# Two attention layers and two SwiGLU layers on one core: Wo's products allowed in the column-tiled form, and TensorE's written-out order changed

## The chip, the cores and the metric

The kernel runs on one core of a Trainium2 chip. The metric is the device time of one execution in microseconds, as a median over runs. A profile is one more execution, with every instruction and DMA packet recorded; matmuls stand under PE, the loads of their stationary operand under PEld.

## The reference, cut to what matters

```
x = x + A(layernorm(x));  x = x + B(layernorm(x))      # twice, same weights both times

A: for each of 64 segments of 32 tokens:               # 2048 tokens, width 576
       h   = concat(mem, segment)                      # 8 memory rows + 32 = 40
       q,k,v = h Wq, h Wk, h Wv                        # 32 heads of 128
       p   = softmax(mask(q k^T / sqrt(128)))          # 40 x 40 for each head
       o   = (p v) Wo                                  # 40 x 576
       mem = o[:8];  out = o[8:]
B: (silu(x w1) * (x w3)) w2                            # 576 -> 4608 -> 576
```

The memory rows make the segments of A a recurrence: a segment's q, k and v need the first eight rows of Wo's result for the segment before. Operands are bf16, sums f32.

## The kernel before

**Steps.** Layer 1's attention runs LAG = 8 segments behind layer 0's, and one step t does segment t of layer 0 and segment t - 8 of layer 1 together (72 steps). Steps 8 to 63 have both layers, so a matmul's moving operand has 2 x 40 = 80 columns; the 8 steps at either end have one, and 40 columns. The FFN (`job`) is done for 128 tokens at a time, four steps' worth, and its pieces are laid between those of attention. In each step the 32 heads go in four groups g of eight.

**The pieces of a group** are nodes that `make_nodes` builds; each has an engine, what it depends on, and the buffers it takes and gives back. TensorE's kinds have a letter each in `KINDS` (line 76): Q and q are the products with Wq and Wk and their tail (576 = 4 x 128 + 64, so the last 64 rows are done apart, as two row tiles side by side); S the scores; T the transposition of the probabilities by TensorE, used in the steps with one layer (with both, a transposing DMA on SP writes PTS from PB); P the product with V (PV); O and o the product with Wo and its tail; X, x, V, v, G, g are those with Wv; F, f, W, w the FFN's; a, b, m, n, p transpositions around the layer norms and the residual. ACT and DVE evict the PSUM banks (`em.qk_ev`, `em.ot_ev` and others), DVE does the softmax with one exponential on ACT, POOL clears PB.

**Wo.** `wo` (line 433) does a group's 8 heads x 4 blocks of 128 of Wo's 576 columns: 32 matmuls that add into the bank y of the step, whose four groups all add into it. `wo_tail` (line 435) does the last 64 columns, the even heads into PSUM partitions 0 to 63 and the odd ones into 64 to 127, two tiles of 64 columns side by side. After the fourth group `y_mem` writes the memory columns of the next step's operand HT, for which the next step's Q and q wait.

**Forms.** Each TensorE node names the forms it allows (`mode`): "full" is the whole 128 x 128 array, "row" two tiles of 64 rows, "col" two tiles of 64 columns, and there are quarter forms for V. Q is "full", q, f and g are "row", S (with two layers) and o are "col"; P, T, F, W, G and the transpositions are "full/col": either. `plan` keeps the forms that all nodes of a run have in common (line 152); when the next node has none of them, the run is closed, all its nodes get the first common form, and a change of form is booked. In "col" `Emitter.mm` (line 623) writes each matmul as a pair: the left 64 columns of the stationary operand at tile position (0, 0), the right 64 at (0, 64), both with the same moving operand. A pair is two matmuls and two weight loads where the full form has one of each.

**The order.** TensorE's order is written out as a string of those letters: `FIRST` (773 nodes, steps 0 to about 15), `FOUR` (208 nodes, four steps and the FFN work that goes with them) repeated 11 times, and `LAST` (664). The letters name kinds; the nodes of a kind are taken in their own order. The other engines' orders follow in `plan`: of what is ready, each takes what can start first, by its table of durations, so they shift when TensorE's order does. The program is fully unrolled.

**The start.** `qk` puts 3 x 4 products of 512 columns with the identity ahead of a step-0 QK whose banks nothing has written yet (u = 0 or 4); each reads one of Wk's four loads. Which of Q and q comes first in the string decides whether the banks are still unwritten.

Of the kernel before, what the change touches and what calls it, by code (L numbers as in the profile page):

```python
# [186 lines left out]
def dve(*ns):  # L187
    return sum(0.065 + n / 960 for n in ns)
# [7 lines left out]
def ew(*ns):  # L196
    return (actc(*ns), dve(*ns))


def ewh(*ns):  # L200
# [2 lines left out]


FIRST = (
    "maqqQqQSqTQQQSqQqqSQTQqSXxVvPPTTOOPoPOooOoQqqqqQQSQVvSqqQQQTQSqqXTSPOPTPOOTooPoxOoQQqqqqQSQvVqSQqQQQSqqTPSTOPoOT"
    "PTOPooOoaQqqQQSQqqVvSqQQQqqqTSQPxTSOPXOToToPPOOooQqqqpQQSVvqqQQnQSFfqqQTQSPfqFSOTFPfWoTOPFTOPoofOoFfqqQQWSFQQqqf"
    "vVqQSTFqfQWQQSqfqFPFTSXfPWTOPOxoTFoPOOffooFVqqvQQWQSQqqfFQqqfFSQTWSPQqfqFQFSTOfPWoTOPFTOPfaOoooFfqqQQvqqSQQWSfVF"
    "qQqQWQTQPqSqTOPbSOxxXTXTPooPOOooQpQQqqqqQSnQSFfqFfQvqVSfFWQqqQfPSFPOOooFfPWOFPofOoFQqqfqQWQSqqqQQQSFSGfgqQQqgfFP"
    "GSWPGfggfFFGOPoOOPWOoooFFffqqQQWSqqQQFvSqfVqQQfFSWqQQqfPPSFFOOPWoOffFPoaoOoWQqqqqQQbSQQQqqSGSgqQQqgPGSOPGggGoPOO"  # L210
    "PooOoQqqqppQQQqvVSSnnQFfqqQQQfqqSFFSPfPwOOWoFPoffFOwPWOooFqqffQQwFWQQqqFSSFffqqQQQQqqwWSSgfGFPGgggGPGOoPOOPWOooo"
    "wFqfqqQQQQSffqqFFSQQwvqVWSFQqqffFQWPwSFffPOPOOowooWFPFOoafQQqqqWSQqqqQQQSwSbQqQgqGSggGPGPOGoPgOPOOooo"
)
FOUR = (
    "QqqqppQvVSQQnnQFqfqFSfqqQQFfqQSWPwPSFffOOowFPWoOPFOooFqfqfQQwQQqqgSWGSFqqfQQQPwQSWFqffqFSGgggGPGPOOwooOPWOooFFqq"
    "ffQQQQSwVvqqfFSQQqqWPFSFfqqfQQwOSWPFFoffPOOWPwOoooFfqqQQqqaSQQqWSQQqqqQQSbwSggGGPGPOggoGPOPOOooo"
)
LAST = (
    "QqqppQQSQqqqvVSQQnqqnQSFPqffQOoSPFOFPwWOFPfooOofQQQqqqfFSwWQQFfqqfFSwWqqQQSGqffgFQFPGgWSwPFggfGOOPoGowPOOooFvfqq"
    "VQQQQSWqqFSFqqffQQQQqqSPwWSFfPOOoWwFffPFPOOooowQWQfqqqFSFfqqQQQWSqqqQQSQbvVVSPwXvxPOPOoOPooOoQQppVqqqQQSqvqnQSnQ"  # L220
    "qffFFQTSqqQTPwFfSPWTOOPFffTFooOPWwOooFffqvVQWFQQqqqQSwSQQfqqFSTFfqqQQWTPwSPFOTOffoPTFoPOOWoowxvXVqqQQFSQqfqqQQSF"
    "QQqqqfQTwPSTSWOPFOffTFPToWoPOwOooFqqfvQQQSQqqfVwWSFFfQqqQTWqSPQQqTOSPbOxooTXPTwPOOooQQpqqqQSqQVvnSqqQQqQSQFfqTFP"
    "STfOPoTOwPTFPOOooofVvqqQQQqqSQQSFfqqFQQSTwqqQTFPffSPOTOwxXooPTFPOOffooFQQqqqqQSQFSfvVqqQQQTqqSQwTPfSOFPFTOwTooPf"
    "POfOooFvVQQqwQqqqSQqqQSQfFTSqQqQfPTSPOOooFTTPPfOOoopwfFFnFwffFFwffFFwwffFfFwFfFwffFfFwFfFwffFFwffFFwffFw"
)
ORDER = FIRST + FOUR * 11 + LAST

# [1 line left out]
class Opt:  # L229

    qk, qkt, sc, tr, pv, wo, wog, vm = 0.0079, -0.0342, 0.0268, 0.1447, 0.0406, 0.2653, 0.0725, 0.1407
# [4 lines left out]
def make_nodes(em, nseg, pools, o=Opt, dma_bw=230e3, load_bw=400e3):  # L236
# [4 lines left out]
    def node(*a, **k):  # L241
        n = Node(*a, **k)
        nodes.append(n)
        return n

    def banks(n=2):
        return [Slot("bank") for _ in range(n)]
# [12 lines left out]
    def load(name, nbytes, prio, fn, deps=()):  # L260
        return node("DMA", nbytes / load_bw, fn, deps=deps, prio=prio, name=name, lat=2.0)
# [7 lines left out]
    ld_o = [load("ldo", kb(1024, 576), g - 6.0, em.load_o(g)) for g in range(NG)]  # L269
# [61 lines left out]
    def paired(t):  # L331

        return role(t) == 1 and both(t) and t + 1 < nst and both(t + 1)
# [12 lines left out]
    def vg_out(t, g, b, deps, row):  # L346

        return [node("AD", (0.56, 0.6), em.v_ev(b[r], row, R64, row, 2 * g + r), deps=deps, prio=t + o.vm + 0.01 * g + (0.05 if row == 0 else 0.0), rel=[b[r]],
                     name="VGe") for r in (0, 1)]
# [12 lines left out]
    def step(t):  # L362
# [6 lines left out]
        mm80 = max(c80 / 2.4 + 2.5, 25.0) / 1000  # L369
# [11 lines left out]
        for g in range(NG):  # L381
            qs, qe = [], []
            for u in (2 * g, 2 * g + 1):
                q = Slot("qkt", users=1)
                b = banks()
                pq = t + o.qk + o.ustep * u
                m_ = node("PE", 32 * mm80, em.qk(t, u, b), deps=hx + hm[:1] + ([ld_h[u // 4]] if t == 0 else []),
                          prio=pq, mode="full", acq=[q] + b, name="QK")
                n = node("PE", 4 * mm80, em.qk_tail(t, u, b), deps=hx + hm + ([ld_h[u // 4]] if t == 0 else []), prio=pq + o.qkt, mode="row",
                         acq=[q] + b, name="QKt")  # L390
                rd += [m_, n]
                me[f"QK{u}"], me[f"QKt{u}"] = m_, n
                for r in (0, 1):
                    qe.append(node("AD", ew(256, 64) if nl == 2 else ew(160), em.qk_ev(t, u, r, q, b[r]), deps=[m_, n], prio=t + o.ustep * u,
                                   rel=[b[r]], name="QKe"))
                qs.append(q)
            s = banks(1)[0]
            sme = Slot("sme")
            pf = t + o.gstep * g
            sc = node("PE", 8 * (0.0312 if nl == 2 else 0.029), em.scores(t, g, qs, s), deps=qe, prio=pf + o.sc, mode="col" if nl == 2 else "full/col", acq=[s, sme], rel=qs, name="SC")  # L400
            a = node("DVE", dve(320), em.sm_add(t, g, s, sme), deps=[sc], prio=pf, rel=[s], name="add")
            m_ = node("DVE", 0.912 if nl == 2 else 0.89, em.sm_max(t, g, sme), deps=[a], prio=pf, name="maxsub")
            c = node("ACT", 0.094 + 320 / 1200, em.sm_exp(t, g, sme), deps=[m_], prio=pf, name="exp")
            pb = Slot(f"pb{g % 2}")
            if g < 2 and t:
                zero = [node("POOL", 0.95, em.pb_zero(pb), deps=zdep[g:g + 1], prio=pf, acq=[pb], name="pbz")]
            else:
                zero = []
            d = node("DVE", 0.623 if nl == 2 else 0.606, em.sm_sum(t, g, sme), deps=[c], prio=pf, name="sum", lat=0.14 if nl == 2 else 0.22)
            w = (1.074 if e else 1.143) if nl == 2 else 0.466  # L410
            pbs = node("DVE", w, em.sm_pb(t, g, sme, pb), deps=[d] + zero, prio=pf, acq=[pb], rel=[sme], name="pb", lat=0.125 if nl == 2 else 0.225)
            pts = Slot("pts")
            if nl == 2 and g < DMA_GROUPS:
                pe_ = [node("DMA", TRD, em.ptd(t, g, pb, pts), deps=[pbs], prio=pf, acq=[pts], rel=[pb], name="TRD", lat=TRL)]
                pts_of[t, g] = pe_[0]
            else:
                bt = banks(nl)
                tr = node("PE", 8 * (0.0258 if nl == 1 else 0.0358), em.ptr(t, g, pb, bt), deps=[pbs], prio=pf + o.tr, mode="full/col", acq=[pts] + bt, rel=[pb], name="TR", lat=0.265)
                pe_ = [node("AD", ew(320), em.pt_ev(t, g, i, b, pts), deps=[tr], prio=pf, rel=[b], name="PTe") for i, b in enumerate(bt)]
                pts_of[t, g] = tr  # L420
            if paired(t):
                hn = [ht_ready[li, s] for s in (t + 1, t + 2) for li in (0, 1) if (li, s) in ht_ready]
                gb, gd = vg_nodes(t, g, hm[:1] + hx + hn, hm[1:])
                vx_ev["VM", t, g] = vg_out(t, g, gb, gd, R64)
            b = banks()
            ot = Slot("ot")
            pv = node("PE", 8 * mm80, em.pv(t, g, pts, b), deps=pe_ + vx_ev["VM", t, g] + vx_ev["VX", t - e, g],
                      prio=pf + o.pv, mode="full/col", acq=b + [ot], rel=[pts], name="PV")
            pvs[t, g] = pv
            if paired(t):  # L430
                vx_ev["VX", t + 1, g] = vg_out(t, g, gb, gd + [pv], 0)
            ote = [node("AD", ew(4 * c80), em.ot_ev(t, g, ab, b[ab], ot), deps=[pv], prio=pf, rel=[b[ab]], name="OTe") for ab in (0, 1)]
            wo = node("PE", 32 * mm80, em.wo(t, g, ot), deps=ote + ([ld_o[g]] if t == 0 else []), prio=t + o.wo + o.wog * g, mode="full",
                      acq=[y] if g == 0 else [], name="WO")
            wot = node("PE", 4 * mm80, em.wo_tail(t, g, ot), deps=[wo], prio=t + o.wo + o.wog * g, mode="col", rel=[ot], name="WOt")
            if g:
                wo.after(wos[0])
            if g:
                wot.after(wots[0])
            wos.append(wo)  # L440
            wots.append(wot)
            me[f"SC{g}"], me[f"PV{g}"], me[f"WO{g}"] = sc, pv, wo
# [950 lines left out]
```

## Time and profile before

| | |
|---|---|
| runs | 2642.74, 2635.89, 2644.21 us; median 2642.74 |
| the profiled execution | 2638.71 us |
| its span, first to last instruction | 2636.9 us |
| mean granted TensorE clock | 0.996 |

The span is what the profile's views divide up. "Busy" of TensorE is the time in which at least one matmul is in flight; each lasts some 200 ns and the next starts long before it ends. In a row of the timeline the first number is the start, the second the time until the last matmul of the row has ended, which overlaps the next row; from the start of one row to the start of the next is the time that the row's work held the engine. A shape such as 128*64 128x80 is rows * columns of the array, then the moving operand.

### The profile page before, as it was taken

The page shows a single profiled execution, that of the slowest core. Times are in us where ns is not written, and L with a number is a line of the kernel's source. Part 1 is how long each engine was busy: PE and PEld are TensorE (multiplying, and loading weights), DVE is VectorE, ACT ScalarE, POOL GpSimd, SP SyncE. Part 2 cuts the span into 40 slices and gives each one's busy share as a digit, 9 for nine tenths or more (in the row PEclk, how much of TensorE's full clock was granted, in tenths as well). Part 3 has the DMA queues.
Part 4 walks back from the last instruction along what each step waited for, and adds up shares of the span by engine and source line. Part 5 has one row for each costly group of instructions (what it writes and reads, how often), then busy time and mean ns, then how long its engine had stood idle before and what let it go on. Part 6 is the DMA issues. An engine that isn't in the chain of part 4 may idle for free.

```text
span 2636.9 us, 134690 instructions
## 1 busy us (share of the span) xinstructions
PE 2574.1 (98%) x60031; PEld 2222.3 (84%) x60031; DVE 2004.5 (76%) x5137; ACT 1264.2 (48%) x3745; POOL 196.7 (7%) x253
## 2 busy tenths in 40 slices
PE   5999999999999999999999999999999999999998
PEld 4788888889888888888888888888888888888886
DVE  4787777887778678777877777787777777777876
ACT  2655553444445454444545444454545445454552
POOL 1100000000000010000001001000100001010000
PEclk9999999999999999999999999999999999999999
DMA  9065755575464656546454654655465464545357
GB/s 324 4 174 135 190 104 147 130 148 139 126 147 115 139 127 155 136 131 151 113 140 116 159 140 128 155 110 139 114 156 143 132 159 94 139 122 146 106 156 247
DMA packets 683207, 371.56 MB, mean 141 GB/s; under 512 B 233753, under 2 KB 672801, under 8 KB 681985
## 3 DMA queue, kind: packets, MB, share of 16 engines
q1 hardware_dynamic: 678944, 355.00, 53.2%
q8 instruction: 469, 7.68, 1.2%
q0 software_dynamic: 3024, 6.93, 0.9%
q10 hardware_dynamic: 656, 1.02, 0.2%
q14 instruction: 114, 0.93, 0.1%
HBM read 306.72 MB, written 2.36 MB: 117 GB/s over the span
## 4 chain that ended last, share of the span: by engine, by line
PE 91%; DVE 4%; DMA 3%; issue 1%; ACT 1%; ACTq 0%; DVEq 0%; SPq 0%
PE bank L627 91%; DMA PTS<-PB 2%; DVE HTT L633 1%; DVE PB L633 1%; DVE STAT L633 1%; DMA WV<-in_A_Wv_dram 0%; DVE SME L633 0%; DMA W<-in_A_Wk_dram 0%; DVE V L633 0%; DVE QKT L633 0%; DMA W2C<-in_B_w_dram 0%; DVE XR L633 0%; ACT HTT L630 0%; ACT HT L630 0%; DVE LNS L633 0%
## 5 line engine op out<-in xcount | busy, mean ns | idle before, releaser
L627 PEld LDWEIGHTS <-W 128*128 128x128 bf16 (+2 forms) x32920 | 1261.8, 101 | 119.8 <-issue 67.8
L627 PE MATMUL bank<-HT,W 128*128 128x80 bf16 (+3 forms) x23040 | 795.2, 197 | 21.3 <-ACT HT L630 8.2
L627 PE MATMUL bank<-XTB,W 128*64 128x256 bf16 (+5 forms) x9880 | 658.4, 264 | 2.1 <-issue 1.3
L630 ACT ACTIVATE QKT<-bank 128x256 bf16<-128x256 f32 (+4 forms) x1676 | 385.1, 309 | 302.9 <-PE bank L627 296.5
L627 PE MATMUL bank<-OT,WO 128*128 128x80 bf16 (+3 forms) x11520 | 411.6, 198 | 2.5 <-issue 1.9
L627 PEld LDWEIGHTS <-WO 128*128 128x128 bf16 (+1 forms) x11520 | 383.2, 102 | 29.9 <-issue 16.3
L630 ACT ACTIVATE V<-bank 64x512 bf16<-64x512 f32 (+1 forms) x603 | 338.0, 584 | 137.4 <-PE bank L627 131.4
L627 PE MATMUL bank<-WV,HT 128*32 128x512 bf16 (+4 forms) x3576 | 363.5, 384 | 0.3 <-issue 0.2
L627 PE MATMUL bank<-W2C,HTT 128*64 128x288 bf16 (+1 forms) x3440 | 323.8, 287 | 0.5 <-DMA W2C<-in_B_w_dram 0.5
L630 ACT ACTIVATE HTT<-bank 128x512 bf16<-128x512 f32 (+1 forms) x322 | 172.6, 551 | 300.1 <-PE bank L627 299.1
L633 DVE TENSOR_REDUCE STAT<-SME 104x8 f32<-104x320 f32 (+1 forms) x576 | 274.9, 477 | 28.2 <-ACT SME L630 21.2
L633 DVE TENSOR_TENSOR PB<-SME,STAT 40x128 bf16<-40x128 f32 (+4 forms) x912 | 274.8, 335 | 9.3 <-DMA PTS<-PB 0.5
L627 PEld LDWEIGHTS <-HT 128*32 128x32 bf16 (+4 forms) x3576 | 149.2, 99 | 147.7 <-issue 37.8
L633 DVE SCALAR_TENSOR_TENSOR HTT<-HTT,bank 128x512 bf16<-128x512 bf16 (+1 forms) x322 | 201.0, 624 | 94.4 <-ACT HTT L630 91.6
L627 PEld LDWEIGHTS <-HTT 128*64 128x64 bf16 (+1 forms) x3512 | 233.1, 106 | 31.2 <-DVE HTT L633 4.1
L1047 POOL MEMSET PB<- 128x1024 bf16 x142 | 135.0, 952 | 1657.0 <-DMA PTS<-PB 1114.3
L633 DVE SCALAR_TENSOR_TENSOR XR<-bank,XR 128x288 f32<-128x288 f32 x574 | 240.0, 447 | 20.3 <-PE bank L627 17.2
L630 ACT ACTIVATE OT<-bank 128x320 bf16<-128x320 f32 (+1 forms) x383 | 144.4, 404 | 214.5 <-PE bank L627 185.3
L630 ACT ACTIVATE SME<-SME 104x320 f32<-104x320 f32 (+1 forms) x288 | 135.5, 470 | 194.3 <-DVE SME L633 192.4
L633 DVE TENSOR_TENSOR HTT<-HTT,bank 128x512 bf16<-128x512 bf16 (+1 forms) x322 | 203.3, 631 | 28.5 <-PE bank L627 1.4
L633 DVE CAST V<-bank 64x512 bf16<-64x512 f32 (+1 forms) x261 | 178.9, 686 | 40.1 <-PE bank L627 34.9
L633 DVE TENSOR_TENSOR SME<-bank,maskb 104x320 f32<-104x320 f32 (+1 forms) x288 | 138.5, 482 | 53.8 <-PE bank L627 50.1
(59 smaller groups left out, 1383.5 us busy)
## 6 DMA issues: line engine op xcount, KB each, us to landing
W<-in_B_w_dram SPq DMA_DIRECT2D x608, 256.0 KB, 3.6
W2C<-in_B_w_dram SPq DMA_DIRECT2D x304, 288.0 KB, 3.4
W<-in_B_w_dram SPq DMA_DIRECT2D x608, 32.0 KB, 3.4
W<-in_B_w_dram SPq DMA_DIRECT2D x8, 1024.0 KB, 12.6
W<-in_A_Wq_dram SPq DMA_DIRECT2D x9, 512.0 KB, 9.9
WO<-in_A_Wo_dram SPq DMA_DIRECT2D x4, 1152.0 KB, 19.1
XR<-in_A_x_dram POOLq DMA_DIRECT2D x16, 288.0 KB, 3.1
WV<-in_B_w_dram SPq DMA_DIRECT2D x4, 1152.0 KB, 7.5
```

The source lines that it names most:

```text
L627: self.ch("PE", self.nc.tensor.matmul(out, lhsT=lhsT, rhs=rhs, start=start, stop=stop, skip_group_check=True, **k))
L630: self.ch("ACT", self.nc.scalar.activation(*a, **k))
L633: self.ch("DVE", getattr(self.nc.vector, fn_)(*a, **k))
L1047: return lambda n: self.ch("POOL", self.nc.gpsimd.memset(self.pbt(pb), 0.0))
```

## The change

One node's list of forms, and the three strings of TensorE's order.

```
-            wo = node("PE", 32 * mm80, em.wo(t, g, ot), deps=ote + ([ld_o[g]] if t == 0 else []), prio=t + o.wo + o.wog * g, mode="full",
+            wo = node("PE", 32 * mm80, em.wo(t, g, ot), deps=ote + ([ld_o[g]] if t == 0 else []), prio=t + o.wo + o.wog * g, mode="full/col",
...
 FOUR = (
-    "QqqqppQvVSQQnnQFqfqFSfqqQQFfqQSWPwPSFffOOowFPWoOPFOooFqfqfQQwQQqqgSWGSFqqfQQQPwQSWFqffqFSGgggGPGPOOwooOPWOooFFqq"
-    "ffQQQQSwVvqqfFSQQqqWPFSFfqqfQQwOSWPFFoffPOOWPwOoooFfqqQQqqaSQQqWSQQqqqQQSbwSggGGPGPOggoGPOPOOooo"
+    "QqqqppQvVSQQnnQFfqqFSqfqQQFfqQSWPwPSFffOoOwoPFWOoPFOoFqqffQQwQQqqgSWGSFfqqQQQPwQSWFqffqFSGgggGPGOPOWoOPFoOwooFfq"
+    "qfQQQQSWVvfqqFSQQqqwPFSFqqffQQOSWwPFFPffOOooWPwOooFfqqQQqqaSQQqqWSQQqqQQSbwSggGGPGPOoggGPOoPOOoo"
...
 FIRST = (
-    "maqqQqQSqTQQQSqQqqSQTQqSXxVvPPTTOOPoPOooOoQqqqqQQSQVvSqqQQQTQSqqXTSPOPTPOOTooPoxOoQQqqqqQSQvVqSQqQQQSqqTPSTOPoOT"
+    "maQqqqQqSQQQTqqSQqSqTQQSvVXxPPTTOoPOoOPoOoQqqvqqQQSQVqqSQQQSqQTqPSTXPTOOPoTOPxooOoQQqqqqQSQVvSqqQQqQSqQTPSTOPoTO"
```

`FIRST` and `LAST` change throughout in the same way. The counts of each kind stay: the same nodes in another order. With the new list, a run of neighbours that holds O and also S or o is no longer closed at O: the whole run, and with it P, F, W, G and T where they stand in it, can take the column form. `wo` itself is not edited; in the column form `Emitter.mm` writes its 32 matmuls as 32 pairs.

More of the change, by code (lines that the diff above doesn't have):

```diff
@@ L205 @@
 FIRST = (
-    "maqqQqQSqTQQQSqQqqSQTQqSXxVvPPTTOOPoPOooOoQqqqqQQSQVvSqqQQQTQSqqXTSPOPTPOOTooPoxOoQQqqqqQSQvVqSQqQQQSqqTPSTOPoOT"
[L207 to L210, printed above, removed]
@@ L211 @@
-    "PooOoQqqqppQQQqvVSSnnQFfqqQQQfqqSFFSPfPwOOWoFPoffFOwPWOooFqqffQQwFWQQqqFSSFffqqQQQQqqwWSSgfGFPGgggGPGOoPOOPWOooo"
-    "wFqfqqQQQQSffqqFFSQQwvqVWSFQqqffFQWPwSFffPOPOOowooWFPFOoafQQqqqWSQqqqQQQSwSbQqQgqGSggGPGPOGoPgOPOOooo"
+    "maQqqqQqSQQQTqqSQqSqTQQSvVXxPPTTOoPOoOPoOoQqqvqqQQSQVqqSQQQSqQTqPSTXPTOOPoTOPxooOoQQqqqqQSQVvSqqQQqQSqQTPSTOPoTO"
+    "PoTOPoaOoQQqqqqQSQVvqqSQQqTQSQqxPTSOPXOToToPPOoOoQqqqpQQSVvqqqQQnSQFfqQTSQPFfqOSTFfPWTOPFooTOPoffOoFQWqqqQQSQqqf"
+    "vVQTFSFQqfqQQSqWPFSXffFTTxWPOTPOoFoPOOooFffvVqqqQQWQSFqqffQFSQWQQqfqqQSTFTfPFSOPWoTOPaFTOPfooOoFfqqQQqqvSQQWSVFf"
@@ L213 @@
+    "QqQqTWqqQQPSTOPboSOxXTXTPxoPOoOoQpQqqqqQQSnQSFfqFfvqQVSFfqQWqQfPSFPFOofOPoWOFfPoOoFQqfqqQQSQQQqqqWSGSFfgqqQQFfgP"
+    "GSWPGFffggFGOoPOWPoOoOoFFqqffQQWqqSQQvFSqfVQQqWSFfqqQQfPPSFOOoFoPWOfFPfoaOoWQqqqqQQbSQQQqqSGSgqQQqgPGSOPGggoGPOO"
+    "PooOoQQppQqqqqQVSSnqvnQFqfqQQQSFqffPFOSWwPoFFffPOoOwPWOooFqqfqQQwQQqWSSffqQFFQQQqqqwSWFgffGSFPGgggGPGOoPOPOFWwoo"
+    "OoFqffqQQQQSwFqfqqQQWqvVSSFqffFQQqwPWSFFffPOOWooPwOPFOoofaQQqqWSqqqQQQQSqwSbQQqqgGSggGPGPOgGoPOPOOooo"
 )
 FOUR = (
-    "QqqqppQvVSQQnnQFqfqFSfqqQQFfqQSWPwPSFffOOowFPWoOPFOooFqfqfQQwQQqqgSWGSFqqfQQQPwQSWFqffqFSGgggGPGPOOwooOPWOooFFqq"
@@ L216 @@
-    "ffQQQQSwVvqqfFSQQqqWPFSFfqqfQQwOSWPFFoffPOOWPwOoooFfqqQQqqaSQQqWSQQqqqQQSbwSggGGPGPOggoGPOPOOooo"
+    "QqqqppQvVSQQnnQFfqqFSqfqQQFfqQSWPwPSFffOoOwoPFWOoPFOoFqqffQQwQQqqgSWGSFfqqQQQPwQSWFqffqFSGgggGPGOPOWoOPFoOwooFfq"
+    "qfQQQQSWVvfqqFSQQqqwPFSFqqffQQOSWwPFFPffOOooWPwOooFfqqQQqqaSQQqqWSQQqqQQSbwSggGGPGPOoggGPOoPOOoo"
 )
 LAST = (
-    "QqqppQQSQqqqvVSQQnqqnQSFPqffQOoSPFOFPwWOFPfooOofQQQqqqfFSwWQQFfqqfFSwWqqQQSGqffgFQFPGgWSwPFggfGOOPoGowPOOooFvfqq"
-    "VQQQQSWqqFSFqqffQQQQqqSPwWSFfPOOoWwFffPFPOOooowQWQfqqqFSFfqqQQQWSqqqQQSQbvVVSPwXvxPOPOoOPooOoQQppVqqqQQSqvqnQSnQ"
@@ L221 @@
[L221 to L224, printed above, removed]
+    "QqqppQQSQqqqvVSQQqqnnQSFfqfPQOSoPFOFPWwOFPofoOofQQQqqfFSwQWQqfqqFSFqqfqQQQWwSSFgfgfGFPGWwOPFgfgGGoPOwPOOoooWVvfq"
@@ new lines @@
+    "qFQQQSQQqfqqFSFqqfqQQQSPwWSfFPFOOWwoPffFPoOOoowWFqfqQQQSFfqqqQQSWqqQQqSQVvVPSbwXvxPOPoOOPooOoQQppVqqqQQSqqvnQSnQ"
+    "qffFFTqQSQPWFTqfwPTOSOFPffFOoooTWPwOoFqqfvVQQWSFQfqqqQwQSFqfqfFQQTSTQWqwPSFOPoTFPTOoPOOooffxXVvqWQQqqqQSQwQSQqqF"
+    "qqffFQSTQWwSTPFTOffPFoPwTOWPoOoOoFvqqfQQQSQfqqVwWSFFfQQqqTWTSqqQPQOoPSbOXToxPTwPOoOoQqqqpQQSQvqVSQnqqQQTfSFQqqFP"
+    "STfPOToOowPTFPOoOofVvqqQQQQSqqQSFqqfqQQFSTwPQffqTOSPFTOXxooPTwPOFOoofFQqqfqQQSQqfVvSFTQQqqQSPqqQwSTFPfFTOOofPwTO"
+    "PooOoFfvVqfQQqwSQqQqqqQSFQQTQqSqSTPPOFfOToTPPOOooopfwfFFnFwffFFwffFFwwfFffFwFffFwFfFwffFFwffFfFwFfFwffFw"
```

## Prediction

> **What bounds the kernel now.** I read the page's engine row first, then the chain that ended last, then TensorE's waits, then its timeline.
>
> ```profile
> PE 2574.1 (98%) x60031; PEld 2222.3 (84%) x60031; DVE 2004.5 (76%) x5137; ACT 1264.2 (48%) x3745; POOL 196.7 (7%) x253
> ...
> q8 instruction: 469, 7.68, 1.2%
> ...
> PE 91%; DVE 4%; DMA 3%; issue 1%; ACT 1%; ACTq 0%; DVEq 0%; SPq 0%
> ```
> ```profile
> PE bank L627 <- issue: 9.2, 15, 1.6
> PE bank L627 <- ACT HT L630: 8.2, 20, 1.9
> PE bank L627 <- DMA W<-in_A_Wk_dram: 6.4, 4, 3.2
> PE bank L627 <- DMA PTS<-PB: 5.0, 11, 1.4
> ```
> ```profile
> 0.00:236.00 236.00, 197.83 (x5760) 164.60 (x5761) 164.60 (x444) 112.92 (x318) 24.20 (x39) 0.96 0.51 163
> 236.00:2365.00 2129.00, 2117.20 (x47778) 1839.63 (x47775) 1634.43 (x4178) 1026.29 (x3083) 156.38 (x195) 1.00 0.56 136
> 2365.00:2636.90 271.90, 259.09 (x6507) 218.11 (x6502) 205.46 (x517) 125.04 (x346) 16.16 (x19) 0.99 0.54 161
> ```
>
> TensorE is busy 98% of the span and holds 91% of the chain. The three stages of the windows view (first number: length; second: PE busy and count) are the steps with one layer at the start, the steps with both, and one layer again: PE idles 38, 12 and 13 us. So what the change does to the length of TensorE's stream, it does to the time, nearly one for one. The row of queue q8 is TensorE's own code: 7.68 MB in 469 packets is 16,384 bytes each, and 469 x 256 = 120,064, against 2 x 60,031 = 120,062 matmuls and weight loads. One packet therefore brings 256 instructions of 64 bytes: a **block** of 128 matmuls with their weight loads. I need this below.
>
> **What the change does to TensorE's order.** I counted both orders by the rule in `plan` (a run of neighbours takes a form that all allow). Before, all 288 WO groups are full. After, 263 are column-tiled: 210 of 80 columns (210 x 32 = 6720 products become pairs) and 53 of 40 columns (1696 pairs). The neighbours they join turn with them: 26 more PV and 13 more TR groups at 40 columns, and at 80 or more columns 121 PV, nearly all VG, and most FF and W2. Changes of form fall from 1269 to 1085. TensorE's matmuls rise from 60,031 to 71,176, so its blocks from 469 to 556. DVE and ACT get the same work, a few evictions of it exchanged between them. SP and POOL issue the same DMAs; on SP 292 places of 985 differ, such as a load of XN that now stands elsewhere among the FFN weights. TensorE's waits on DMAs behind the start are the 5.0 us for PTS in the row above, and I put this reordering at nothing, between losing the 5.0 and doubling it.
>
> **Term 1: changes of form.**
>
> ```profile
> 1164.20 1.91 PE L627 MATMUL bank<-XTB,W 128*64 128x256 bf16 x32
> 1165.95 0.45 PE L627 MATMUL bank<-PTS,V 128*64 128x80 bf16 x16
> 1166.23 1.15 PE L627 MATMUL bank<-W2C,HTT 128*64 128x288 bf16 x16
> 1167.22 1.56 PE L627 MATMUL bank<-OT,WO 128*64 128x80 bf16 x40
> 1168.61 0.45 PE L627 MATMUL bank<-PTS,V 128*128 128x80 bf16 x8
> 1168.90 1.91 PE L627 MATMUL bank<-XTB,W 128*128 128x256 bf16 x16
> 1170.65 1.72 PE L627 MATMUL bank<-OT,WO 128*128 128x80 bf16 x48
> 1172.20 1.92 PE L627 MATMUL bank<-XTB,W 128*64 128x256 bf16 x32
> 1174.05 0.32 PE L627 MATMUL bank<-HT,W 64*128 64x80 bf16 x8
> 1174.20 0.38 PE L627 MATMUL bank<-XTB,W 64*128 64x256 bf16 x4
> 1174.42 0.31 PE L627 MATMUL bank<-HT,W 64*128 64x80 bf16 x8
> 1174.56 0.38 PE L627 MATMUL bank<-XTB,W 64*128 64x256 bf16 x4
> 1174.87 2.47 PE L627 MATMUL bank<-HT,W 128*128 128x80 bf16 x64
> 1177.18 1.15 PE L627 MATMUL bank<-W2C,HTT 128*128 128x288 bf16 x8
> ```
>
> Matmuls overlap, so I measure from one row's start to the next row's, never by the busy time. FF in columns, followed by its own form: 1165.95 - 1164.20 = 1.75; followed by row tiles: 1174.05 - 1172.20 = 1.85. FFt without a change behind it 0.22, with one 0.31. A change costs 0.09 to 0.10; I take 0.095. 184 fewer: **-17.5 us**. The first pairs after a change are slower too: WO's 48 rows, 32 full and 16 in 8 pairs, take 1.55 = 32 x 0.036 + 0.095 + 8 x 0.035 + 0.02, and 64 full ones after a change 2.31 instead of 2.30. 45 fewer entries into columns at 0.02 and 135 fewer into full at 0.01: **-2.2 us**.
>
> **Term 2: a pair against a full product.** At 80 columns PV takes 0.28 for 8 pairs (35 ns) and 0.29 for 8 full (36 ns); FF 1.75 in both forms. So 6720 WO pairs cost nothing more, as long as a run goes on like its first 8 pairs. At 40 columns it differs:
>
> ```profile
> 2525.51 0.35 PE L627 MATMUL bank<-ident,PB 104*128 104x40 bf16 x8
> 2525.71 1.05 PE L627 MATMUL bank<-XTB,W 128*128 128x128 bf16 x16
> ...
> 2527.74 0.96 PE L627 MATMUL bank<-OT,WO 128*128 128x40 bf16 x32
> 2528.54 0.35 PE L627 MATMUL bank<-ident,PB 104*128 104x40 bf16 x8
> ...
> 2532.79 0.43 PE L627 MATMUL bank<-OT,WO 128*64 128x40 bf16 x16
> 2533.07 0.41 PE L627 MATMUL bank<-PTS,V 128*64 128x40 bf16 x16
> 2533.32 0.41 PE L627 MATMUL bank<-ident,PB 104*64 104x40 bf16 x16
> 2533.57 1.06 PE L627 MATMUL bank<-XTB,W 128*64 128x128 bf16 x32
> ```
>
> Full: 0.80 / 32 = 25 ns, and 0.20 for 8. Column pairs: 0.25 / 8 = 31 ns. 1696 x 6 ns = 10.2, and 39 groups of PV and TR x 0.05 = 2.0: **+12.2 us**. Terms 1 and 2 together: -17.5 - 2.2 + 12.2 = **-7.5 us**.
>
> At the start the first QK now opens its banks itself, and so brings 12 more warm-up products:
>
> ```profile
> 32.47 2.89 PE L627 MATMUL bank<-W,ident 128*128 128x512 bf16 x12
> ```
>
> They cost 0 to 2.9 us; I take 0, because they stand where TensorE waits 6.4 us for Wk (row above), each behind one of its four loads.
>
> **Term 3: the supply of instructions.** This one decides. In the last stage the timeline shows waits that no semaphore explains:
>
> ```profile
> 2538.00 0.27 PE L627 MATMUL bank<-OT,WO 128*64 128x40 bf16 x6 [0.82 <-issue]
> 2538.12 1.06 PE L627 MATMUL bank<-XTB,W 128*64 128x128 bf16 x32
> 2539.11 2.20 PE L627 MATMUL bank<-HT,W 128*128 128x40 bf16 x90
> 2541.75 1.15 PE L627 MATMUL bank<-HT,W 64*128 64x40 bf16 x38 [0.44 <-issue]
> ```
>
> Between the two waits stand 6 + 32 + 90 = 128 matmuls, exactly one block. TensorE had run out of code, got a block at 2538.00, and although it idled again at the end it had the next one only at 2541.75: a starved block costs **3.75 us**. A block of full products of 80 columns lasts 128 x 0.036 = 4.6 us, and the middle stage's mean block 2129 / (47778 / 128) = 5.7 us, so the supply is just covered there. A block of column pairs of 80 columns does the same work in 64 pairs = **2.3 us**: 1.4 us short. The changed order has runs such as POoPOOoo, 124 pairs of 80 columns in a row (two blocks), in each of 11 repeats; before, the longest such run is 24 pairs.
>
> I laid both orders out at the rows' prices (0.095 a change, 36 and 31 ns a pair) and cut them into blocks. Taking each block by itself, 33 blocks of before fall short of 3.75 us, by 12.3 us together; if two neighbours may share, by 5.2. The trace has 9.2 (the row "issue"), in between. After: 158 blocks, by 128 us alone and 84 shared (38 in the first stage with its 31 ns pairs, 26 in the 11 repeats, 20 in the last). Added: 128 - 9.2 = 118 at most, 84 - 9.2 = 74 at least by this count; placed as before's 9.2 lies, 99. I take 87, nearer the shared end, since most short blocks of the repeats have a long neighbour to share with. While TensorE starves, the other engines catch up, so waits of the other two kinds go: 8.2 + 5.0 = **-13**. Sum: -7.5 + 87 - 13 = **+66 us**.
>
> [...]
>
> [...]
>
> The profiled execution took 2638.71 us (span 2636.9 and 1.8 around it); the median of the runs is 2642.74, between 2635.89 and 2644.21, so the base may be off by 4. 2638.7 + 66 = **2705 us**.
>
> **Rivals.**
> - *Changes of form alone.* The supply keeps up after all: -7.5, **2631 us**, the side of faster. For it: in 2129 us of the middle stage PE idles 12 us, and 3.75 was measured while data DMAs ran; against it: the waits 128 matmuls apart. It decides where a starved block takes 2.6 us or less: the shared count is then about 5 us and the single one 17, which the saved changes pay. Chance 0.10; half of it beyond 0.3% (7.9 us), which is about what a measurement of this kernel can tell from no change. [...]
> - *Slow pairs.* A long run is held by its weight loads, two of 31 ns one after the other, 62 ns a pair: 6720 x 26 ns = +175 on top of -7.5, **2806 us**. Against it: 35 ns in 8 pairs. It loses from 37 ns a pair on. Chance 0.03.
> - *Half covered.* Deeper buffering in the repeats, the added wait is 0 to 15 us: within 8 us of before, **2639 us**. Chance 0.03. It needs the 26 us of the repeats gone and most of the 40-column waits with them; but if eight neighbours shared, the count is still 24 against 1.2, so +15 and 2654, which I count to the forecast's low end.
> - *Forecast*, supply-bound in short blocks: chance 0.84, between 2654 and, with all 118 us and no wait saved, 2749; with blocks at 4.2 us more.
>
> **Numbers.** Faster by over 0.3%: 0.05 (half of the first rival). Within: 0.05 + 0.03 = 0.08. Slower: 0.84 + 0.03 = 0.87. The range, 2652 to 2760, leaves out the first rival, the slow pairs, and the ends of the forecast.
>
> **What would show it.** Right: the row "issue" among TensorE's waits grows from 9.2 to 70 us or more, the waits lie 128 matmuls apart, behind runs of WO in 128*64 form; PE's share falls below 97%; packets of q8 near 556; the timeline still has 35 to 36 ns a pair inside WO at 80 columns and 31 at 40. Wrong: "issue" stays near 9 and the span drops by 7 to 8 (the first rival), or WO's pairs run at 40 ns or more with no gaps (slow pairs). The size fails if blocks starve at other than 3.75 us in the middle stage, where data DMAs are as busy as anywhere (0.56).

## The result, and the profile after

The changed kernel takes 2739.46 us (median, 2735.73 to 2744.64) against 2641.94 us for the kernel before (2635.89 to 2644.21): a ratio of 1.0374, with a 95% interval from 1.0349 to 1.0399, or 97.5 us more. The forecast was 2705, its range 2652 to 2760. The profiled execution took 2735.73 us with a span of 2733.9, 97.0 us over the span of before.

From the page of after, the engine row, the row of q8 and the chain, each to be held against its row of before:

```profile
PE 2609.5 (95%) x71173; PEld 2275.5 (83%) x71176; DVE 2007.0 (73%) x5137; ACT 1268.2 (46%) x3745; POOL 196.7 (7%) x253
...
q8 instruction: 556, 9.11, 1.4%
...
PE 91%; issue 3%; DMA 3%; DVE 2%; ACT 1%; SPq 0%; ACTq 0%; DVEq 0%
```

TensorE was idle for 2636.9 - 2574.1 = 62.8 us before and is for 2733.9 - 2609.5 = 124.4 us after: 61.6 of the 97 us are idle time of the engine that sets the end. The other engines have the same work in more time. TensorE's waits in after say what it waits for (in total, times, longest):

```profile
PE bank L627 <- issue: 71.1, 86, 2.8
...
PE bank L627 <- DMA W<-in_A_Wk_dram: 6.6, 2, 4.3
PE bank L627 <- ACT HT L630: 6.4, 20, 0.3
...
PE bank L627 <- DMA PTS<-PB: 2.9, 6, 1.1
```

"Issue", the wait that no semaphore explains, went from 9.2 us in 15 waits to 71.1 us in 86 (+61.9), as much as the added idle time. HT and PTS fell by 3.9 us together. The groups by their shapes show whose waits these are (the last column is idle time ahead of the group, and its releaser). Wo's products of 80 columns before:

```profile
L627 PE MATMUL bank<-OT,WO 128*128 128x80 bf16 x7168 | 285.2, 202 | 0.2
```

Wo's column pairs after, with the pairs of its tail:

```profile
L627 PE MATMUL bank<-OT,WO 128*64 128x80 bf16 x15232 | 319.3, 202 | 24.9 <-issue 21.1 <-DVE V L633 2.2
L627 PE MATMUL bank<-OT,WO 128*64 128x40 bf16 x3904 | 85.9, 194 | 23.4 <-issue 23.3
```

44 of the 71 us stand ahead of Wo's column pairs themselves. How far apart the waits lie is seen in the timeline of after, in one of the repeats:

```profile
438.92 1.05 PE L627 MATMUL bank<-OT,WO 128*64 128x80 bf16 x47 [0.43 <-issue]
439.77 1.18 PE L627 MATMUL bank<-W2C,HTT 128*64 128x288 bf16 x16
440.75 0.48 PE L627 MATMUL bank<-PTS,V 128*64 128x80 bf16 x16
441.03 1.18 PE L627 MATMUL bank<-W2C,HTT 128*64 128x288 bf16 x16
442.01 0.77 PE L627 MATMUL bank<-OT,WO 128*64 128x80 bf16 x33
443.21 1.05 PE L627 MATMUL bank<-OT,WO 128*64 128x80 bf16 x47 [0.42 <-issue]
```

47 + 16 + 16 + 16 + 33 = 128 matmuls between two waits: one block, and 4.29 us. The same in the first stage, where the pairs have 40 columns:

```profile
191.74 1.29 PE L627 MATMUL bank<-OT,WO 128*64 128x40 bf16 x70 [0.80 <-issue]
192.87 1.06 PE L627 MATMUL bank<-XTB,W 128*64 128x128 bf16 x32
193.77 0.28 PE L627 MATMUL bank<-OT,WO 128*64 128x40 bf16 x8
193.89 0.41 PE L627 MATMUL bank<-PTS,V 128*64 128x40 bf16 x16
194.14 0.19 PE L627 MATMUL bank<-OT,WO 128*64 128x40 bf16 x2
197.11 2.65 PE L627 MATMUL bank<-OT,WO 128*64 128x40 bf16 x128 [2.78 <-issue]
200.84 0.56 PE L627 MATMUL bank<-OT,WO 128*64 128x40 bf16 x14 [1.08 <-issue]
```

Blocks of 5.37 and 3.73 us. In all, the trace has 27 places where two waits of the row "issue" stand 128 matmuls apart; they last from 3.45 us, 4.3 in the median, and 95% of them up to 5.3. With the waits that are too short for that row there are 37 such places, 4.0 us in the median. Most other distances between such waits are multiples of 128, or one or two matmuls short of one: TensorE's queue also holds some 110 semaphore instructions, which would account for that.

The three stages of after, by windows (length; PE busy and count; the other engines; granted clock, DMA share, GB/s):

```profile
0.00:236.00 236.00, 192.50 (x6105) 159.91 (x6108) 143.81 (x387) 98.44 (x271) 21.70 (x36) 0.89 0.47 153
236.00:2365.00 2129.00, 2078.59 (x55637) 1828.15 (x55636) 1603.66 (x4100) 1010.99 (x3026) 152.04 (x189) 1.00 0.56 133
2365.00:2733.90 368.90, 338.45 (x9445) 287.39 (x9439) 259.49 (x651) 158.72 (x450) 22.94 (x28) 0.97 0.50 144
```

The stretches are those of before, so their ends cut the work elsewhere. Two things are to be seen: in the middle stretch TensorE idles 50 us instead of 12, and in the outer ones the granted clock fell, from 0.96 to 0.89 and from 0.99 to 0.97. The prediction had not foreseen the second.

To share out the 97 us I took, over the whole trace, the time from each matmul's start to the next one's and set it against what is usual for that form at full clock. What exceeds it by over 0.3 us is a wait; the rest belongs to a change of form, to half clock, or to the products themselves. In us:

| | before | after | difference |
|---|---|---|---|
| waits of TensorE | 84.6 | 173.0 | +88.4 |
| lost to half clock, waits apart | 2.6 | 10.9 | +8.3 |
| changes of form, beyond the usual distance | 109.6 | 87.8 | -21.8 |
| the products themselves | 2425.7 | 2448.2 | +22.5 |
| ahead of the first matmul | 10.7 | 10.1 | -0.6 |

The waits are larger here than in the row "issue" because that row starts to count where the last matmul has ended, about 0.2 us after the next could have started. Which of the first two rows a wait at half clock is put under is a matter of counting: a second count, with the mean distance of each form as the usual one, gives +80 and +16 for them and -22 and +24 for the next two. The first two rows are surer as a sum than each by itself.

### The profile page after: what moved, and what is told of

It is laid out like the page before. It is cut to its first block, busy times and chain, and to the rows that moved or that the text cites. A ratio compares the mean times of both kernels' runs of the same rounds, so it can differ in the third digit from the quotient of the medians.

```text
span 2733.9 us, 156952 instructions
## 1 busy us (share of the span) xinstructions
PE 2609.5 (95%) x71173; PEld 2275.5 (83%) x71176; DVE 2007.0 (73%) x5137; ACT 1268.2 (46%) x3745; POOL 196.7 (7%) x253
## 4 chain that ended last, share of the span: by engine, by line
PE 91%; issue 3%; DMA 3%; DVE 2%; ACT 1%; SPq 0%; ACTq 0%; DVEq 0%
PE bank L627 91%; DMA PTS<-PB 1%; DMA W<-in_B_w_dram 1%; DMA W<-in_A_Wk_dram 1%; DVE HTT L633 1%; DVE V L633 0%; DVE PB L633 0%; DVE STAT L633 0%; DMA XN<-in_A_x_dram 0%; DVE SME L633 0%; DMA W2C<-in_B_w_dram 0%; DVE QKT L633 0%; ACT HT L630 0%; ACT HTT L630 0%; DVE OT L633 0%
## 5 line engine op out<-in xcount | busy, mean ns | idle before, releaser
L627 PE MATMUL bank<-XTB,W 128*64 128x256 bf16 (+5 forms) x10232 | 667.3, 265 | 9.0 <-issue 6.3
L630 ACT ACTIVATE QKT<-bank 128x192 bf16<-128x192 f32 (+4 forms) x1678 | 383.4, 310 | 280.8 <-PE bank L627 276.5
L627 PE MATMUL bank<-OT,WO 128*64 128x80 bf16 (+2 forms) x19936 | 434.2, 200 | 48.3 <-issue 44.4
L627 PEld LDWEIGHTS <-WO 128*64 128x64 bf16 (+1 forms) x19936 | 409.1, 114 | 68.0 <-issue 63.0
L627 PE MATMUL bank<-WV,HT 128*64 128x512 bf16 (+3 forms) x4070 | 365.5, 387 | 1.2 <-issue 1.2
L627 PEld LDWEIGHTS <-HT 128*64 128x64 bf16 (+3 forms) x4072 | 156.6, 102 | 149.3 <-issue 45.8
L627 PEld LDWEIGHTS <-HTT 128*64 128x64 bf16 (+1 forms) x4096 | 246.8, 109 | 28.4 <-issue 5.0
```

The lines of the kernel that those rows point to most:

```text
L627: self.ch("PE", self.nc.tensor.matmul(out, lhsT=lhsT, rhs=rhs, start=start, stop=stop, skip_group_check=True, **k))
L630: self.ch("ACT", self.nc.scalar.activation(*a, **k))
```

## The experiments

**Theory:** TensorE runs out of instructions wherever a block of 128 matmuls has less array time than the supply of a block takes; the column form hurts because it makes two instructions of one. **Rivals:** the new order is to blame; or the column form is slow in itself.

**The form alone.** The kernel before, with the order that it had, and one word changed:

```
-            wo = node("PE", 32 * mm80, em.wo(t, g, ot), deps=ote + ([ld_o[g]] if t == 0 else []), prio=t + o.wo + o.wog * g, mode="full",
+            wo = node("PE", 32 * mm80, em.wo(t, g, ot), deps=ote + ([ld_o[g]] if t == 0 else []), prio=t + o.wo + o.wog * g, mode="full/col",
```

> The order of before, with Wo allowed the column form (the one line of the diff outside the order): 247 of 288 WO products go in columns, 70,160 matmuls in 548 blocks of 128, 1092 changes of form. Supply theory: the count of short blocks at 3.75 us is 130 us alone and 82 shared (after 128 and 84), so as slow as after: about 2730 us (2715 to 2745), TensorE's wait 'issue' 60 to 80 us. Rival, the new order is to blame: the form alone only saves changes, 2631 to 2645 us, 'issue' near 9 us. Rival, slow column pairs: near 2730 too, but without gaps, 'issue' near 9 and more than 36 ns a pair in the timeline.

2746.75 us (2735.24 to 2749.05), ratio 1.0387, interval 1.0363 to 1.0410: as slow as after (2 us above the expected range). TensorE's first wait in it:

```profile
PE bank L627 <- issue: 75.5, 100, 2.4
```

The loss needs no new order. By the shares of the table above: waits +94, half clock +5, changes -19, products +17.

**The order alone.** After, with that word changed back.

> The order of after, with Wo held to full products: 60,355 matmuls in 471.5 blocks, 1417 changes of form instead of 1269. Supply theory: the changes cost 148 x 0.095 = 14 us, pairs of PV and TR fall back to full, the short blocks amount to 10.3 us alone and 3.7 shared (before 12.3 and 5.2): 2650 to 2660 us, 'issue' 5 to 12 us. Rival, the new order is to blame: 2690 us or more.

2663.31 us (2662.10 to 2667.18), ratio 1.0082, interval 1.0067 to 1.0097: 21 us over before and 3 above the expected range. By the shares, waits +0.5 and changes +15 (148 more), products +6, half clock +2.5; "issue" is 7.7 us. An order made for the column form is worth little without it, but it isn't what costs 97 us.

**Half the pairs' instructions.** After, in which a pair of Wo's issues its left half alone (the first product of a step excepted), so that half of Wo's result is left out:

```
+                    first = g == 0 and hl == 0 and db == 0
+                    if n.mode == "col" and not first:
+                        self.mm(yT[0:R64, db, :], self.T.WO[:, self.head(g, hl), db * P:db * P + R64], OT[:, hl, :], False, False,
+                                tile_position=(0, 0))
+                        continue
...
```

> After, with the right 64 columns of Wo's column products left out (all but the first of a step), so that each pair is one instruction pair fewer: the same order, the same changes of form, and the same time in the array if the two columns of a pair run side by side, but 62,700 matmuls in 490 blocks instead of 71,152 in 556. This leaves out half of the Wo products. Supply theory: the short blocks fall to 14.5 us alone and 7.1 shared, 'issue' to 8 to 18 us, and the time to 2631 to 2655 us. Rival, the column form itself is slow (weight loads, or the way its products stand): the time stays at 2700 us or more with few instructions too. Rival, a column costs by itself and not by the pair: the 263 products would run in half their time and the time would fall by over 100 us below before.

2641.80 us (2638.98 to 2647.15), ratio 0.9998, interval 0.9988 to 1.0007. The profile of this kernel, its waits and its two groups of Wo's columns:

```profile
PE bank L627 <- issue: 8.2, 10, 2.9
```
```profile
L627 PE MATMUL bank<-OT,WO 128*64 128x80 bf16 x8554 | 311.8, 202 | 1.5 <-issue 0.9 <-ACT OT L630 0.3
L627 PE MATMUL bank<-OT,WO 128*64 128x40 bf16 x2215 | 79.3, 191 | 1.2 <-issue 1.0
```

This speaks against both rivals. Order, forms and changes of form are those of after; the groups are still in flight for 311.8 us with 8554 matmuls instead of 319.3 with 15,232, so one column takes the time of a pair, and the column form is not slow in itself. The number of instructions fell, with it the work of the right 64 columns, and "issue" went from 71.1 to 8.2 us and the time down by 98 us.

**The supply by itself.** All of the computation is left out. Stages of 16 blocks of one product each (the calls are set several to a line here); a pair has `tile_position=(0, 0)` and `(0, 64)`. This kernel and the two others of products alone were run once each.

```
    stage(80, False, 16); stage(80, True, 16); stage(128, True, 16)     # columns, in pairs, blocks
    stage(40, False, 16); stage(40, True, 16); stage(512, False, 1)
    traffic(18); stage(80, True, 16); stage(512, False, 1)
    traffic(18); stage(80, False, 16)
```

> All of the computation is left out; TensorE runs stages of 16 blocks of 128 matmuls each on data that lies there, with nothing that waits for another engine: full products of 80 columns, column pairs of 80, column pairs of 128, full of 40, column pairs of 40, and then, with 18 loads of FFN weights running, column pairs of 80 and full of 80. Supply theory: a block of column pairs of 80 takes 3.4 to 3.8 us instead of the 2.3 us of its array time, with a gap at each block's end and 35 ns a pair inside; the pairs of 40 the same 3.4 to 3.8 us instead of 2.0; full products of 80 take 4.6 us without gaps and pairs of 128 3.6 us with almost none; full ones of 40 3.3 to 3.8. With loads running the pairs take 3.8 to 4.5 us a block. Rival, slow column pairs: the pairs of 80 are slow evenly, over 40 ns each, without gaps. Rival, the supply keeps up: 2.3 us a block. The granted clock: if starvation brings half speed, the stages of pairs have a lower clock than those of full products; otherwise both have 1.00 after the start.

The timeline of that kernel, from its full products of 80 columns into the pairs, and later full products of 40 columns and the pairs under the loads:

```profile
17.21 79.86 PE L627 MATMUL bank<-WO,W 128*128 128x80 bf16 x2271 [17.21 <-DMA WO<-in_A_Wo_dram]
97.91 2.48 PE L627 MATMUL bank<-WO,W 128*64 128x80 bf16 x128 [0.84 <-issue]
101.91 2.48 PE L627 MATMUL bank<-WO,W 128*64 128x80 bf16 x128 [1.52 <-issue]
105.36 2.48 PE L627 MATMUL bank<-WO,W 128*64 128x80 bf16 x128 [0.97 <-issue]
...
149.01 68.01 PE L627 MATMUL bank<-WO,W 128*64 128x80 bf16 x2432 [1.52 <-issue]
217.38 6.82 PE L627 MATMUL bank<-WO,W 128*128 128x40 bf16 x256 [0.36 <-issue]
224.56 6.82 PE L627 MATMUL bank<-WO,W 128*128 128x40 bf16 x256 [0.36 <-issue]
...
361.26 2.48 PE L627 MATMUL bank<-WO,W 128*64 128x80 bf16 x128 [2.09 <-issue]
...
426.57 28.57 PE L627 MATMUL bank<-WO,W 128*64 128x80 bf16 x163 [1.53 <-issue]
```

Full products of 80 columns run without a wait (under the loads with a single one, of 0.23 us). The pairs wait at every 128th matmul: 14 blocks in 149.01 - 97.91 = 51.1 us, 3.65 us a block, of which the pairs themselves take 2.3. With the loads, 14 blocks take 426.57 - 361.26 = 65.3 us, 4.66 a block (some of it half clock, below), more than the 4.5 expected at most. Pairs of 128 columns (in the row from 149.01) have next to no waits, as expected. Full products of 40 columns, 3.3 us a block in the array, wait too: 12 blocks take 261.36 - 217.38 = 44.0 us, 3.67 a block. So it is a block's array time that counts, and not the column form.

The trace also has the time of each packet of q8, and these show where the 3.65 us go. There is one packet for each block (114 for 14,596 matmuls), and no two are under way at once. In the 14 blocks of pairs from 97.91 on, the packet of the next block starts 1.0 to 1.6 us after the first matmul of the running one (1.1 in the median), takes 0.9 to 1.4 us (1.0), and the next block's first matmul comes 1.3 to 1.5 us after the packet's end (1.4). With the loads only the first of the three parts grows in the median, to 2.1 us. So a block's supply is one fetch at a time, 1.1 + 1.0 + 1.4 = 3.5 us by the medians from one block's first matmul to the next one's, and while a block runs only the packet of the next one comes; bandwidth is not what is short (DMA share 0.02 in the quiet stage, in the windows below).

**Only the two-layer steps.** After, with Wo free in the steps of 80 columns alone: `mode="full/col" if nl == 2 else "full"`.

> After, with Wo held to full products in the steps of one layer (40 columns) and free in those of two (80 columns): 210 WO products in columns, 68,987 matmuls, 1157 changes of form. The short blocks at 3.75 us: 42 us shared, 82 alone. Supply theory: 26 of the 42 lie in the repeats, whose added time stays at about 28 us as in after, and the first and last stage give back most of what they lost, in waits (first stage 38 to 13 us shared, last 20 to 4) and in granted clock (0.994 or more instead of 0.986): 2665 to 2690 us, 'issue' 35 to 55 us. Rival, the 80-column runs do no harm and all is due to the 40-column form: 2630 to 2645 us. Rival, what costs is the new order in the first and last stage: 2720 us or more.

2697.22 us (2688.15 to 2704.48), ratio 1.0213, interval 1.0187 to 1.0238: 55 us of the 97 stay, above the expected range by 7. By the shares, waits +53, half clock +4, products +10, changes -13. "Issue" is 47.2 us in 76 waits. So the steps of both kinds pay: more than half of the loss comes from pairs of 80 columns, and the granted clock of the first stage is back at 0.97.

**Few pairs, chosen.** The order of before, with Wo allowed the column form in the two-layer steps; the forms are chosen for the whole order at once, each instruction more at a price:

```
+            more = EXTRA.get(n.name, 5) if m == "col" and "full" in n.forms else 0
+            row[m] = best[src[m]] + (0.11 if src[m] != m else 0.0) + lam * more
...
+    reform(order, 0.005, 0.002)
```

> The order of before. Each of TensorE's products that can take both forms has its form chosen for the whole order at once, with 0.11 us for a change and 5 ns (first and last stage) or 2 ns (repeats) for each instruction pair more; WO may go in columns in the steps of two layers. 49 of 288 WO products do, 61,106 matmuls in 477 blocks, 1227 changes of form instead of 1269. Supply theory: changes -4 us, pairs at 40 columns that turn full -2, short blocks 4.6 us shared and 19 alone (before 5.2 and 12.3), so 2630 to 2645 us, the same or up to 8 us faster. Rival, any WO in columns costs about as after's do (97 us for 263): 49 would add 18 us.

2642.51 us (2634.20 to 2649.77), ratio 0.9998, interval 0.9986 to 1.0010, "issue" 7.6 us. 49 groups of Wo in columns, chosen so, do no harm (the rival had 18 us more), and the 4 us of changes don't show. No version here beats the kernel before.

**What a neighbour lends.** Only products again, pairs (64 are 128 matmuls, 2.3 us) and full ones (128, 4.6 us) in turn, the borders of the blocks 32 matmuls further in each stage; then pairs of 72, 64, 56 and 40 columns:

```
    ...
    for phase in range(4):
        for _ in range(8):
            for _ in range(64):
                mm(80, True)
            for _ in range(128):
                mm(80, False)
        for _ in range(32):
            mm(80, False)
    for cols in (72, 64, 56, 40):
        stage(512, False, 1)
        stage(cols, True, 16)
    ...
```

> All of the computation is left out. First four stages of 8 periods of 64 column pairs (128 matmuls) and 128 full products, all of 80 columns, 6.9 us of array time a period; the stages differ in where the borders of the blocks fall, 32 matmuls further in each. Only one block is fetched ahead, theory of a block by itself: where the borders fall between the two forms a period takes 4.6 + 3.65 = 8.2 us, and where they halve them 2 x 3.65 = 7.3 us. Theory of sharing (the count at the low end of the prediction): 7.3 us at every place of the borders. Then column pairs of 72, 64, 56 and 40 columns, 16 blocks each, after a block of 512 columns: 3.65 us a block each; the clock falls to half where the array is used too little, between 64 and 40 columns (pairs of 80, used 0.58 of the time, kept 1.00, pairs of 40 fell to 0.50). Rival on the clock: it fell for the length of the whole starved stretch, and 72 columns fall too.

A period has 7.1 us of array time and takes 7.40, 7.24, 7.48 and 7.35 us in the four stages. In the last, where the borders fall between the forms, the timeline has

```profile
219.90 36.66 PE L627 MATMUL bank<-WO,W 128*64 128x80 bf16 x1280 [0.25 <-issue]
256.73 14.56 PE L627 MATMUL bank<-WO,W 128*64 128x80 bf16 x512 [0.17 <-issue]
271.45 37.45 PE L627 MATMUL bank<-WO,W 128*64 128x80 bf16 x512 [0.17 <-issue]
```

7 periods of 256 matmuls in 271.45 - 219.90 = 51.55 us: 7.36, not 8.2. A short block between long ones borrows from its neighbour. How much, the next one asks, with k short blocks and 2k long ones:

```
    ...
    for k_ in (1, 2, 4, 8):
        for _ in range(16 // k_ if k_ < 8 else 3):
            stage(80, True, k_)
            stage(80, False, 2 * k_)
    ...
```

> All of the computation is left out. Column pairs and full products of 80 columns again, now k blocks of pairs (2.3 us of array time each) followed by 2k blocks of full products (4.6 us each), for k = 1, 2, 4 and 8: on the mean 3.8 us a block, which a supply of 3.65 us a block covers if enough blocks can lie ready. How many do, by the loss for each run of k short blocks: if three blocks are held (the one that runs, and two), none at k = 1 and 2, 1.6 us at k = 4 and 6.9 us at k = 8; if four, none, none, none and 3.3 us; if eight, none anywhere; if two, 1.3, 2.6, 5.3 and 10.6 us.

The timeline: all of k = 1 in the first row, then the first two periods of k = 2 and one of k = 4:

```profile
17.04 212.19 PE L627 MATMUL bank<-WO,W 128*128 128x80 bf16 x6879 [17.04 <-DMA WO<-in_A_Wo_dram]
230.08 23.38 PE L627 MATMUL bank<-WO,W 128*64 128x80 bf16 x768 [0.85 <-issue]
254.10 23.38 PE L627 MATMUL bank<-WO,W 128*64 128x80 bf16 x768 [0.64 <-issue]
...
422.89 2.48 PE L627 MATMUL bank<-WO,W 128*64 128x80 bf16 x128 [0.97 <-issue]
426.36 2.48 PE L627 MATMUL bank<-WO,W 128*64 128x80 bf16 x128 [0.99 <-issue]
429.83 41.73 PE L627 MATMUL bank<-WO,W 128*64 128x80 bf16 x1280 [0.99 <-issue]
```

From start to start the k short blocks take no longer than their array time at k = 1, and 0.95, 3.85 and 9.2 us longer (means) at k = 2, 4 and 8. No whole number of held blocks fits (two would give 2.6, 5.3, 10.6; three 0, 1.6, 6.9). In this kernel the borders cut a run of k blocks of pairs into a mixed block, 0.75 us short of 3.65, and k - 1 full ones, 1.37 short each: 2.1, 4.9 and 10.3 us. So about 1.1 us is lent to a run, whatever its length and however many long blocks stand before it. The packets fit: in a block of full products the next one's packet starts 0.2 us after the first matmul (median of 109 blocks), in one of pairs 1.1 us (41 blocks), so a run of pairs starts with its fetch about 0.9 us ahead of those that follow.

## Why the prediction was right, and where its sizes were off

**Term 3, the supply, decides:** shown. "Issue" grew to 71.1 us (70 or more was forecast), the waits stand 128 matmuls apart behind Wo's columns, PE's share fell to 95%, q8 has 556 packets, and with half the pairs' instructions left out all of it goes. The packets themselves say the same: 83 of the 86 waits end 1.2 to 1.7 us after a packet of q8 has ended (so do all 15 of before), while the waits of other kinds stand anywhere between. That the supply keeps up, as *changes of form alone* has it, doesn't hold in the runs: with products alone, 14 blocks of pairs with nothing else to wait for take 3.65 us each instead of 2.3. That rival and *half covered* fall with the time; *slow pairs* falls with the packets, and with the timeline of after, where a run of 32 pairs goes on as its first 8 did:

```profile
2417.68 1.32 PE L627 MATMUL bank<-OT,WO 128*64 128x80 bf16 x64
2418.83 0.46 PE L627 MATMUL bank<-PTS,V 128*64 128x80 bf16 x16
```

1.15 us for 32 pairs is 36 ns each. The 62 ns of *slow pairs* were an estimate: 31 ns is what a whole pair of 40 columns took, both its weight loads included, and no run shows a load that holds up a pair for 31 ns.

**The size of term 3** came out right: waits rose by 88.4 us in all, with HT and PTS 3.9 lower, so by some 92 for all the others, which is the supply but for about 1 us, where 87 was forecast. But two errors nearly cancel in it, so its size is partly luck. A starved block was put at 3.75 us, from one place of the last stage; after has 4.0 to 4.3 in the median. The prediction's own sign that the size fails, blocks at other than 3.75 us in the middle stage, came: 11 blocks between waits there take 4.55 us in the median, as their packets start 2.0 us after the first matmul instead of 1.1. And "two neighbours may share" lets a short block take all that it lacks from a long neighbour, where a run of them gets about 1.1 us once. Counted with 4.0 us and 1 us lent, the orders give 8 us for before, 101 for after, 103 for the form alone, 6 for the order alone and 50 for the two-layer steps; the differences, +93, +95, -2 and +42, stand against measured waits of +88, +94, +0.5 and +53. This count was made after the results, and its 4.0 is read from the trace that it explains; only the 1 us was measured apart from them. It leans on the 4.0: a coarser count along the matmuls of after gives some 85 us with it, and some 35 with the 3.65 and 1.1 us of the products alone.

**"Waits of the other two kinds go, -13":** the step of the sum that failed most. HT and PTS went from 13.2 to 9.3 us, 3.9 less. TensorE's starving doesn't take those waits away: HT has 20 of them before and after. The 3.9 us need no starving either: with the order alone HT has 6.9 us and PTS 2.0, 4.3 less than before.

**Terms 1 and 2, -7.5 us:** +0.7 by the shares (-21.8 and +22.5). The changes are as forecast (-19.7, entries included). The products cost 10 us more than the 12.2 forecast. Two parts can be read off the trace: a pair of 80 columns takes 36.2 ns against 35.9 on the mean of all its runs, 2 us for 6640 of them, and pairs of 40 take 32.2 against 25.4, 1 us more than forecast. The rest is spread over the forms and isn't settled.

**Not in the sum:** granted clock, 8 us. So 66 becomes 97 by +9 for the waits of other kinds, +8 for the clock, +8 for terms 1 and 2, and +5 for term 3 (66 + 30 = 96, and 1 of rounding). The part of starving in the lower clock is shown below for the products alone; in after it is argued from where it lies, the two outer stages. With half the pairs' instructions left out the last stage is back at 0.99, the first only at 0.93 of the 0.96 of before: there, about half of the lost clock stays without the starving, and its cause is open.

## What to carry to other kernels

Where TensorE is the bound, count its instructions by blocks of 128 matmuls and lay their array time against what a block's supply takes (3.65 us in a quiet kernel, 4.0 to 4.6 here): a form that doubles the matmuls for the same array time is free only while the blocks stay above that. A change of form at 0.095 us is cheaper than a block of 80-column pairs that starves, 1.4 us or more. So a run of 128 such matmuls should not be made for the sake of the changes it saves; short runs next to long products did no harm here, but brought no measured gain either. To tell it from other causes, look for waits "issue" that stand 128 matmuls apart, to within two, and that end soon after a packet of TensorE's instruction queue; and leave out half the instructions at the same array time.

## What the runs showed of the hardware that was not expected

Starving can bring half clock, though no wait for instructions in the two kernels here is longer than 3.2 us. In the kernel of the supply by itself, by windows: the pairs of 80, those of 40 from 280 us on, and the pairs of 80 under loads (granted clock, DMA share and GB/s are the last three):

```profile
97.00:149.00 52.00, 34.85 (x1795) 33.08 (x1792) 0.00 (x0) 0.00 (x0) 1.00 0.02 4
280.00:320.00 40.00, 38.37 (x1382) 37.57 (x1384) 0.00 (x0) 0.00 (x0) 0.50 0.02 5
361.00:427.00 66.00, 40.85 (x1816) 39.07 (x1818) 0.00 (x0) 0.00 (x0) 0.90 0.80 227
```

And the pairs of 72, 64, 56 and 40 columns in the kernel of the four stages:

```profile
310.00:364.00 54.00, 33.76 (x1832) 31.41 (x1833) 0.00 (x0) 0.00 (x0) 1.00 0.02 5
395.00:448.00 53.00, 32.83 (x1831) 30.63 (x1832) 0.00 (x0) 0.00 (x0) 1.00 0.02 5
480.00:534.00 54.00, 33.85 (x1816) 31.58 (x1811) 0.00 (x0) 0.00 (x0) 0.97 0.02 5
565.00:618.00 53.00, 45.50 (x1792) 44.18 (x1792) 0.00 (x0) 0.00 (x0) 0.61 0.02 4
```

Without loads all are starved alike, at some 3.7 us a block; the clock gives way as the columns get fewer, from 56 on, and with 80 columns when loads stretch a block to 4.66 us. Pairs of 64 and of 40 columns are in flight equally long, 2.21 us a block at full clock, with waits alike (0.97 to 1.80 us with 64, 1.14 to 1.54 with 40 until the clock falls), and yet 64 keep 1.00: so it is not the idle time that decides here, but how many columns go through the array. An estimate of how much that fills: from 330 to 355 us of the kernel of the supply by itself, 118 products of 512 columns take 25.00 us at full clock, 0.414 ns a column; at that price the 64 pairs of a block fill 0.58 of 3.65 us with 80 columns, 0.46 with 64, 0.41 with 56 and 0.29 with 40. At half clock a block of pairs of 40 columns takes 3.8 us (3.75 before the clock fell), so the slower clock costs next to nothing while the supply is the bound; the changed kernel, with longer products between the pairs, loses 10.9 us to half clock, waits apart, by the shares above (before 2.6). In the pairs of 40 the clock went to half after waits of 1.1 to 1.5 us, with TensorE at work in between. By the granted clock in windows of 5 us, the stretches at half clock in the kernel of the supply by itself are multiples of 3.4 us: one of about 51 us from the pairs of 40 on, and four of 3.4 us in the pairs of 80 under loads.
